# State update of a gated recurrence on Trainium2: 48 columns in place of 64 in the stationary operand and the output

## The chip, the cores and the metric

The kernel runs on one core of one Trainium2 chip. The metric is the time of one execution on the device in microseconds (us), the median over several executions. The core has five engines that work side by side, each on an instruction stream of its own: TensorE (PE in the profile; its weight loads, LDWEIGHTS, are listed apart as PEld), VectorE (DVE), ScalarE (ACT), GpSimd (POOL) and SyncE (SP), which here issues the DMA transfers. TensorE multiplies a stationary operand, which a load puts into its array, by a moving operand that streams through it, and writes to PSUM, a small memory that the other engines read from.

## The reference

Two layers follow each other: a gated linear recurrence over 4 batches, 8 heads, 768 tokens and head size 48, and a feed-forward block with a hard-swish gate.

```python
def _attn_ref(q, k, v, alpha):          # each (4, 8, 768, 48)
    for t in range(S):
        state = alpha[:, :, t, :, None] * state + np.einsum('bhd,bhe->bhde', k[:, :, t], v[:, :, t])
        y[:, :, t] = np.einsum('bhd,bhde->bhe', q[:, :, t], state)
    return y

def _moe_ref(x, w_in, w_out):           # x (3072, 384), w_in (384, 2048), w_out (2048, 384)
    h = x @ w_in
    g = h * np.clip(h + 3.0, 0.0, 6.0) / 6.0
    return g @ w_out
```

The state of each head is a 48 x 48 matrix. Everything is float32.

## The kernel before, in words

**Chunks.** The recurrence is worked in 24 chunks of 128 tokens (6 per batch, numbered j). Within a chunk the running products of alpha are folded into q and k, so that a chunk needs only matrix products: scores of q against k within each half of 64 tokens (`scores`, line 346), their product with v and the contribution of the state carried in (`attend`, line 455), and the update of the state by the chunk's k and v (`update`, line 429).

**Two heads to a tile.** The 128 partitions of the k and q tiles hold two heads: head a of a pair occupies rows 64a to 64a+47, and the 16 rows behind it are padding, with k zero there. There are NP = 4 pairs p. `kb_t[j]` is k turned round: 128 tokens on the partitions, and for each pair 128 columns, which are again 48 columns of head 0, 16 of padding, 48 of head 1 and 16 of padding. For the first chunks the turning is done by TensorE (`k_by_token`, line 374, copied by ScalarE in line 378), later by a DVE block transpose and a trip through DRAM (`turn_k`, `write_k`, `read_k`, lines 388 to 405; buffer `far`).

**The update.** `update(j, *at)` computes u = k^T v for each half b of the chunk's tokens, each pair p and each head a. The stationary operand is 64 tokens x 64 columns of `kb_t[j]`, the moving operand is 64 tokens x 48 columns of v, and the output goes to 64 partitions of a PSUM bank, one bank per half. A call issues 16 such products (8 in the last chunk of each batch, where only one half is needed). They use a quarter of the array each: rows 64b to 64b+63 and columns 64a to 64a+63, written 64*64 in the profile. Since the operands are float32, each product becomes two weight loads and two matmuls: 32 of each per call, 704 of each in all.

**What reads u.** `next_state(j, b)` (line 439, line 437 for the first half of a batch) adds u, read over all 128 partitions, to the state on VectorE: first to `half_st` (named s in the profile), then to `sm`. Only rows 64a to 64a+47 of the states are read after that: `place_state` (line 419) copies them beside v, where `attend` uses them. `decayed_state` (line 409, GpSimd) makes `st` out of `sm`.

**The feed-forward block.** It works on groups of two chunks, 256 tokens. The first groups use plain products (`ff1`, line 478; `ff1_half`, line 489; `ff2`, line 516). Later ones use schemes with fewer products and more additions: `product1` (line 600) and `product` (line 703) on TensorE, with the sums before and after on VectorE (lines 537 to 541, 647, 664, 723), copies on ScalarE (lines 606, 682, 709) and the gate on both (lines 494 and 498).

**Order.** The whole order is written out by hand in one string of steps (from line 755), such as `u.16.0.3` for the update of chunk 16 into banks 0 and 3; nothing is reordered by a scheduler. Each engine takes its instructions in that order and waits on semaphores where a buffer or an operand isn't ready.

Of the kernel before, what the change touches and what calls it, by code (L numbers as in the profile page):

```python
# [17 lines left out]
def kernel(  # L18
# [32 lines left out]
    nc = tc.nc  # L51
    B, H, S, D = q.shape
# [26 lines left out]
    half = consts.tile([C, 1], FP, tag="half")  # L79
# [141 lines left out]
    R_t, P_t, Q_t, K_t, kb_t, A_t, xT_t, ps_t = ({} for _ in range(8))  # L221
# [200 lines left out]
    def update(j, *at):  # L422
        for b, i in enumerate(at):
            ps_t["u", j, b] = banks[i][:, 0 : NP * D].rearrange("r (p n) -> r p n", p=NP)
        for p in range(NP):
            for a in range(2):
                for b in range(len(at)):
                    half = slice(HB * b, HB * b + HB)
                    nc.tensor.matmul(ps_t["u", j, b][64 * a : 64 * a + 64, p],  # L429
                                     kb_t[j][half, p, 64 * a : 64 * a + 64],  # L430
                                     v_t[j][half, b, 2 * p + a, 0:D],
                                     start=True, stop=True)

# [189 lines left out]
    def hidden1(g, o):  # L623
# [16 lines left out]
    b = {(i, k): w2[:, i * HF : (i + 1) * HF, k * HD : (k + 1) * HD]  # L640
         for i in range(2) for k in range(2)}
# [83 lines left out]
    def store2(g, i):  # L725
# [13 lines left out]
        "sc": scores, "m": masked, "qa": place_q, "kb": k_by_token, "ck": keep_k,  # L739
        "st": decayed_state, "sv": place_state, "kt": turn_k, "kw": write_k, "kr": read_k,  # L740
        "u": update, "sm": next_state, "ya": lambda j, i: attend(j, 0, i),
        "yb": lambda j: attend(j, 1), "cy": keep_x,
        "f": ff1, "fa": lambda i, m: ff1_half(0, i, m), "fb": lambda i: ff1_half(1, i, None), "fr": gate, "fg": hidden, "b": ff2, "bo": keep_out, "so": store, "x": combine_w2,
# [195 lines left out]
```

## Time and profile before

| | us |
|---|---|
| median of 3 executions | 539.71 (539.61 to 539.85) |
| profiled execution, first to last instruction (the span) | 538.1 |
| median less this span | 1.6 |
| line 429, matmuls, busy (704) | 16.7 |
| line 429, weight loads, busy (704) | 14.2 |
| line 346, matmuls, busy (768) | 16.7 |
| line 455, matmuls, busy (1536) | 25.5 |
| line 600, matmuls, busy (1600) | 209.1 |
| line 703, matmuls, busy (1232) | 213.7 |

The profile shows one execution; of the time outside its span nothing is recorded. Busy time is the union of the records of a group, so records that overlap are counted once: a matmul of line 429 lasts some 220 ns from the start of its record to the end, but 704 of them take up only 16.7 us, since many are in flight at the same time. The spacing of starts, not the length of one, tells how fast they follow each other. The granted TensorE clock is 1.0 throughout.

### The profile page before, as it was taken

What the parts mean: (1) busy time and instruction counts of PE and PEld (TensorE: products, weight loads), DVE (VectorE), ACT (ScalarE), POOL (GpSimd) and SP (SyncE); (2) the same over time, 40 slices, a digit from 0 to 9 for tenths busy, and PEclk for the clock granted to TensorE, in tenths of its full rate; (3) what the DMA queues carried; (4) which work ended last, traced back from release to release, by engine and by line L of the source; (5) the groups of instructions that cost most, each with busy time, mean ns of one, the idle gap of its engine ahead of it and who ended that gap; (6) DMA issues with size and microseconds to landing.
All of it is one profiled execution on the core that took longest, in us unless ns stands there. A gap on an engine that the chain in (4) does not pass through costs nothing.

```text
span 538.1 us, 15166 instructions
## 1 busy us (share of the span) xinstructions
PE 526.3 (98%) x6306; PEld 499.7 (93%) x6306; DVE 475.3 (88%) x839; ACT 259.6 (48%) x513; POOL 50.4 (9%) x71
## 2 busy tenths in 40 slices
PE   8799999999999999999999999999999999999997
PEld 7688886789999999999999999999999999999996
DVE  6999989999999899989999898999999898495481
ACT  3889865212653553543544444642644544553230
POOL 5333425100000000000010000000000000000000
PEclk9999999999999999999999999999999999999999
DMA  9998876006625156263444355155354042100001
GB/s 172 211 251 250 218 217 154 17 2 154 149 35 117 30 117 141 46 140 86 94 109 112 89 121 137 21 127 120 88 136 103 15 103 42 44 3 1 15 16 37
DMA packets 124101, 54.40 MB, mean 101 GB/s; under 512 B 83329, under 2 KB 116865, under 8 KB 124033
## 3 DMA queue, kind: packets, MB, share of 16 engines
q1 hardware_dynamic: 124032, 53.44, 43.7%
q8 instruction: 49, 0.80, 0.7%
q14 instruction: 20, 0.16, 0.1%
HBM read 44.50 MB, written 8.91 MB: 99 GB/s over the span
## 4 chain that ended last, share of the span: by engine, by line
PE 83%; DVE 10%; DMA 3%; ACT 1%; issue 1%; SPq 0%; POOL 0%; DVEq 0%; ACTq 0%; POOLq 0%
PE m_ps L703 32%; PE m_ps L600 32%; PE m_ps L478 6%; PE t_ps L455 4%; PE t_ps L346 2%; PE t_ps L429 2%; DMA v<-in_v_dram 2%; PE m_ps L532 1%; PE m_ps L489 1%; PE m_ps L516 1%; DVE rings L647 1%; DVE R L309 1%; DVE raw L537 1%; DVE g_sb L647 1%; DVE w L537 1%
## 5 line engine op out<-in xcount | busy, mean ns | idle before, releaser
L703 PE MATMUL m_ps<-w,g_sb 128*128 128x192 f32 x704 | 122.1, 327 | 0.6 <-ACT m_ps L709 0.5
L606 ACT COPY g_sb<-m_ps 128x512 f32<-128x512 f32 x110 | 63.5, 584 | 114.7 <-PE m_ps L600 98.2
L703 PEld LDWEIGHTS m_ps<-w,g_sb 128*128 128x128 f32 x704 | 113.7, 190 | 1.7 <-ACT m_ps L709 0.8
L703 PE MATMUL m_ps<-rings,g_sb 128*128 128x192 f32 x528 | 91.6, 327 | 0.6 <-ACT u L682 0.6
L703 PEld LDWEIGHTS m_ps<-rings,g_sb 128*128 128x128 f32 x528 | 85.3, 190 | 1.0 <-ACT u L682 0.9
L600 PE MATMUL m_ps<-xc,w 128*128 128x128 f32 x640 | 82.7, 277 | 0.2 <-DVE w L541 0.2
L600 PEld LDWEIGHTS m_ps<-xc,w 128*128 128x128 f32 x640 | 77.5, 192 | 1.4 <-issue 0.4
L494 ACT ACTIVATE r<-g_sb,half 128x512 f32<-128x512 f32 x80 | 56.7, 722 | 29.4 <-DVE g_sb L541 11.7
L498 DVE SCALAR_TENSOR_TENSOR g_sb<-r,g_sb 128x512 f32<-128x512 f32 x80 | 53.6, 682 | 7.5 <-ACT r L494 7.0
L600 PE MATMUL m_ps<-xT,raw 128*128 128x128 f32 x400 | 52.6, 278 | 0.9 <-ACT g_sb L606 0.9
L600 PEld LDWEIGHTS m_ps<-xT,raw 128*128 128x128 f32 x400 | 48.6, 192 | 1.9 <-ACT g_sb L606 1.2
L409 POOL TENSOR_TENSOR st<-sm,R 128x192 f32<-128x192 f32 x20 | 12.9, 643 | 355.8 <-DVE sm L439 306.7
L647 DVE TENSOR_TENSOR g_sb<-g_sb 128x512 f32<-128x512 f32 (+1 forms) x55 | 42.0, 792 | 1.4 <-PE m_ps L703 1.1
L600 PE MATMUL m_ps<-xT,w 128*128 128x128 f32 x320 | 42.0, 276 | 0.0
L600 PEld LDWEIGHTS m_ps<-xT,w 128*128 128x128 f32 x320 | 39.3, 192 | 0.1
L366 ACT COPY A<-q 48x256 f32<-48x256 f32 x88 | 35.6, 404 | 4.9 <-DVE q L332 3.7
L356 DVE TENSOR_TENSOR A<-t_ps,mask 64x256 f32<-64x256 f32 x96 | 36.1, 414 | 0.4
L478 PE MATMUL m_ps<-xT,w 128*128 128x256 f32 x144 | 32.8, 382 | 0.0
L600 PE MATMUL m_ps<-xc,raw 128*128 128x128 f32 x240 | 31.8, 276 | 0.0
L309 DVE TENSOR_TENSOR_SCAN R<-t,ones 128x516 f32<-128x516 f32 x24 | 29.5, 1231 | 1.3 <-ACT t L300 1.2
L478 PEld LDWEIGHTS m_ps<-xT,w 128*128 128x128 f32 x144 | 26.7, 190 | 3.6
L600 PEld LDWEIGHTS m_ps<-xc,raw 128*128 128x128 f32 x240 | 29.6, 192 | 0.1
(105 smaller groups left out, 730.0 us busy)
## 6 DMA issues: line engine op xcount, KB each, us to landing
raw<-in_moe_w_out_dram SPq DMA_DIRECT2D x8, 768.0 KB, 4.8
raw<-in_moe_w_in_dram SPq DMA_DIRECT2D x6, 768.0 KB, 7.0
v<-in_v_dram SPq DMA_DIRECT2D x48, 96.0 KB, 3.2
out_dram<-oh SPq DMA_DIRECT2D x44, 96.0 KB, 1.8
far<-kq SPq DMA_DIRECT2D x64, 64.0 KB, 2.2
kb<-far SPq DMA_DIRECT2D x64, 64.0 KB, 2.0
aq<-in_alpha_dram SPq DMA_DIRECT2D x36, 96.0 KB, 2.6
qq<-in_q_dram SPq DMA_DIRECT2D x36, 96.0 KB, 2.5
```

The costliest lines, as they stand in the source:

```text
L309: nc.vector.tensor_tensor_scan(out=reverse(R, n - 1, n), data0=reverse(ax, n, n), data1=reverse(ones, n, n), initial=0.0, op0=ALU.mult, op ...
L356: nc.vector.tensor_tensor(out=to[:, a], in0=sc[a][half], in1=mask[half, half].unsqueeze(1).to_broadcast([HB, NP, HB]), op=ALU.mult)
L366: nc.scalar.copy(out=to[:, a], in_=Q_t[j][64 * a : 64 * a + D, :, half])
L409: nc.gpsimd.tensor_tensor(out=st, in0=sm, in1=R_t[j][:, :, 0:1].to_broadcast([C, NP, D]), op=ALU.mult)
L455: nc.tensor.matmul(y_of(j, (i + 1) // 2, p)[:, HB * b : HB * b + HB], vb[:, p, e : e + 32], A_t[j][:, b, 2 * p + a], start=(b == 0 and i = ...
L478: nc.tensor.matmul(h[:, f], w1[:, kk, o : o + C], xT_t[g][:, kk], start=(kk == 0), stop=(kk == KT - 1))
L494: nc.scalar.activation(out=to, in_=h, func=AF.Relu, bias=half, scale=1.0 / 6.0)
L498: nc.vector.scalar_tensor_tensor(out=to, in0=r, scalar=1.0, in1=h, op0=ALU.min, op1=ALU.mult)
L600: nc.tensor.matmul(acc[g][i][:, f * C : (f + 1) * C], spots[w][:, f * C : (f + 1) * C], x_of(g, x), start=(first and f == 0), stop=last, s ...
L606: nc.scalar.copy(out=slots[z], in_=acc[g][i])
L647: nc.vector.tensor_tensor(out=out, in0=in0, in1=in1, op=ALU.subtract)
L703: nc.tensor.matmul(to[g], a, rhs[:, f], start=(first and f == 0), stop=(last and f == HF - 1), skip_group_check=True)
```

## The change

In `update`, the stationary operand becomes 48 of the 64 columns, and the output 48 of the 64 partitions. The moving operand, the number of products, their order, the array quarter that each uses and every other line are as before.

```diff
@@ -426,8 +426,8 @@
             for a in range(2):
                 for b in range(len(at)):
                     half = slice(HB * b, HB * b + HB)
-                    nc.tensor.matmul(ps_t["u", j, b][64 * a : 64 * a + 64, p],
-                                     kb_t[j][half, p, 64 * a : 64 * a + 64],
+                    nc.tensor.matmul(ps_t["u", j, b][64 * a : 64 * a + D, p],
+                                     kb_t[j][half, p, 64 * a : 64 * a + D],
                                      v_t[j][half, b, 2 * p + a, 0:D],
                                      start=True, stop=True)
```

D is 48. The 16 partitions behind each head keep in PSUM what an earlier product left there; `next_state` still reads and adds them, and nothing reads those rows of the state.

## The prediction, made before the changed kernel ran

> **What bounds the kernel now.** I read the page first: engine shares, then the chain of work that ended last.
>
> ```profile
> PE 526.3 (98%) x6306; PEld 499.7 (93%) x6306; DVE 475.3 (88%) x839; ACT 259.6 (48%) x513; POOL 50.4 (9%) x71
> ...
> PE 83%; DVE 10%; DMA 3%; ACT 1%; issue 1%; SPq 0%; POOL 0%; DVEq 0%; ACTq 0%; POOLq 0%
> ```
>
> TensorE is busy nearly always, and 83% of the chain is its work. A shorter TensorE instruction is therefore worth something, provided that it lies on the chain and that its spacing, not only its length, gets shorter. The busy time by stretch says where VectorE could take over (columns: stretch, its length, then busy us and count of each engine, clock, DMA share, GB/s):
>
> ```profile
> 90.00:130.00 40.00, 39.77 (x332) 32.54 (x331) 39.72 (x63) 9.47 (x23) 2.50 (x4) 1.00 0.22 50
> 130.00:190.00 60.00, 59.84 (x855) 58.16 (x854) 57.40 (x107) 31.79 (x66) 2.92 (x4) 1.00 0.41 92
> ...
> 200.00:282.00 82.00, 82.00 (x1042) 80.42 (x1041) 77.97 (x141) 37.89 (x80) 2.68 (x4) 1.00 0.46 103
> 282.00:440.00 158.00, 157.10 (x2049) 154.29 (x2049) 148.48 (x271) 73.71 (x158) 5.04 (x9) 1.00 0.43 97
> ```
>
> From 90 to 130 us VectorE is full (39.72 of 40.00 us), and there the chain runs on it. From 130 to 440 us TensorE is full and VectorE has 4 to 6% left (77.97 of 82.00, 148.48 of 158.00).
>
> Then the changed line, by groups (operands as array rows*columns and out partitions x moving columns; busy us, mean ns of one), with the two lines nearest to it in shape:
>
> ```profile
> L346 PE MATMUL t_ps<-q,k 48*64 48x64 f32 x768 | 16.7, 223 | 0.1
> L429 PE MATMUL t_ps<-v,kb 64*64 64x48 f32 x704 | 16.7, 220 | 1.8 <-ACT kb L378 1.0 <-DMA v<-in_v_dram 0.5 <-issue 0.3
> ...
> L455 PEld LDWEIGHTS t_ps<-A,v 128*32 128x32 f32 x1536 | 22.4, 110 | 3.8 <-DVE s L439 1.0 <-issue 0.7 <-ACT A L366 0.6
> L429 PEld LDWEIGHTS t_ps<-v,kb 64*64 64x64 f32 x704 | 14.2, 134 | 4.3 <-issue 2.9 <-DMA v<-in_v_dram 0.7
> ```
>
> A load of 32 columns lasts 110 ns, one of 64 lasts 134, and one of 128 (line 703) lasts 190: 0.8 ns a column, so the load's length goes by columns.
>
> Last, two calls in the chain in order of time (start, us, what):
>
> ```profile
> 201.21 0.62 PE t_ps L346 x32
> 201.83 0.45 PE t_ps L429 x32
> 202.29 1.76 PE m_ps L600 x14
> ...
> 324.95 0.61 PE t_ps L429 x32
> 325.56 0.48 PE t_ps L346 x32
> ```
>
> The update sits in the chain between other TensorE work, with no wait on either side: what it loses in length, the next line starts earlier.
>
> **The change, part by part.** It adds and removes no instruction and no wait and moves none; on DVE, ACT, POOL and SP nothing differs. The 704 loads of line 429 bring 48 columns instead of 64, and the 704 matmuls have 48 output columns of the array active. `next_state` reads the same 128 partitions, so its 0.35 us stays.
>
> *What one round costs now.* I looked at the single records of the call at 324.88 us. Matmuls start in bursts of four, 6.6 ns apart (one for each quarter of the array), and a burst follows the one before after 58.4 ns: the first of each start at 324.975, 325.033, 325.092, 325.150, ... 325.325, six rounds in 350 ns. With 32 matmuls a call has 8 rounds. The one-half calls (16 matmuls, two quarters) have 8 rounds of 58.4 ns too, so the round belongs to a quarter's own load and matmul, not to the number in flight.
>
> *What sets the 58.4 ns.* Rows with one array quarter, column strip or whole array give spacings by the single records: moving 192 columns 162.7 ns (line 703), 256 columns 216 (line 478), 384 columns 323 (line 516). That is 0.835 ns a column plus 2.5, and gives 56 for 64 columns: line 455, with moving 64 and loads of 32, shows 55.9. Line 346 has the same 64 moving columns but loads of 64, and its round is 58.4. Line 429 moves only 48 columns, for which the matmul line gives 42.5, and its round is 58.4 as well. Line 600 moves 128 (109.5 by the matmul line) and loads 128: 111.7. So two rows that share loads of 64 share 58.4, and loads of 128 give 111.7: (111.7 - 58.4) / 64 = 0.833 ns a column plus 5. I take the load as what sets line 429's round. A load of 48 then gives 40 + 5 = 45.0 ns, just above the matmul's 42.5. Each round saves 13.3 ns, each call 8 x 13.3 = 107 ns.
>
> *Bounds of that saving, since no row has a load of 48.* Best: the round falls to the matmul's 42.5, 15.9 ns x 8 = 127 ns a call; for that the load's 5 ns would have to vanish, which lines 346 and 600 both show. Worst among the harmless ends: a load of 48 costs as one of 64, 0 ns. I take 107, on the line through 64 and 128, from which 48 is 16 columns away.
>
> *How many calls count.* Of the 24 calls, the chain holds 19: those near 34, 45 and 73 us, and 16 from 142 to 468 us. Not in it are 13, 20, 95, 110 and 446 us, where the chain runs on DVE, DMA or ACT. Where it leaves TensorE after 130 us (190 us, over a v load issue and a k transfer through DRAM; 438 us, over ScalarE's copy, a store and the read of k), it does so from a TensorE instruction, so what was saved up to there is carried across, if the transfers start earlier with their issue. The three early calls feed the stretch from 93 to 128 us that VectorE fills; I count them half. Sum: 16 x 107 + 3 x 53 = 1.71 + 0.16 = 1.87 us. The profiled span of 538.1 becomes 536.2; the median shown, 1.6 us above that span, becomes 537.8.
>
> *What hides the rest.* The five calls off the chain are costed at nothing, covered by VectorE's sums (95, 110), by waits for transfers and small DVE work (13, 20) and by ScalarE (446). Were that cover absent, they would add 5 x 107 = 0.53 us. VectorE is next in line: from 130 to 440 us it has 4 to 6% free and the edit takes 15 x 0.107 = 1.6 us, 0.5%, from TensorE's time there, so it doesn't become the bound on average.
>
> **The rivals.**
>
> *Issue sets the round, no gain or almost none.* Line 455 sustains 256 records (loads and matmuls) at 55.9 ns for eight, 7.0 ns a record, and no row keeps a faster pace for long; a round of 45.0 would need 5.6. If 55.9 is a floor, a call saves 2.5 x 8 = 20 ns, 19 calls 0.38 us: 539.3. If the load is rounded to its 64-column quarter: 539.7. For it: no row of this kernel goes below 55.9. Against it: 55.9 is just what 64 moving columns explain, and within a burst eight records start in some 27 ns, 3.4 ns each. The Trainium skill ("TensorE: Matmul & The Clock Gate", sections "Wait — 56ns, not 53.3ns?" and "Back-to-back issue gap") has a rule of this kind: matmul starts never come closer than about 25 ns, however few columns. By that rule over the whole engine 32 matmuls would take an estimated 800 ns a call and narrower loads would bring nothing, 539.7; this trace has 32 starts in 0.46 us and 6.6 ns within a burst, so the rule can only hold for one quarter of the array, where 45 ns is above it.
>
> *The stops outside TensorE take it back.* If the transfer at 190 us (3.16 us in the chain) and the one at 440 us (1.75 us) landed at times of their own, only the call at 468 us would stay: 539.6. Their issue stands behind instructions that wait for TensorE, and DMA shares are 0.51 and 0.23 there, which speaks against it.
>
> *Slower: a partly filled strip breaks the overlap of the quarters.* 48 columns fill one 32-column strip and half of another. If two quarters that share rows could then no longer load side by side, a round would hold two loads, 2 x 45 = 90 ns, 32 more than now: 8 x 32 x 19 calls = 4.8 us, 544.5. It decides as soon as a round is above 58.4 ns. Nothing in the trace has a partial column count; line 346 has partial rows (48 of 64) and keeps its overlap, which speaks weakly against.
>
> **How the numbers follow.** Forecast, the load by columns: 0.76, 537.8, with its own range from 537.0 (all 24 calls at 107 ns and the early ones whole is 2.56; somewhat more with the bound of 127) to 538.6 (six tenths of the 1.87 carried). Issue or rounding: 0.11, 539.3 to 539.7. Stops: 0.05, 539.6. Slower: 0.08, 544.5. 0.2% is 1.1 us, about what a measurement of this kernel can tell from no change: faster by more is the first case, 0.76; within is the second and third, 0.16; slower is 0.08. The range 537.0 to 539.7 reaches over the first three cases.
>
> **What would show it.** Right: bursts of line 429 some 45 ns apart, its loads near 121 ns (134 less 13), its matmuls' busy time down by some 24 x 0.107 = 2.5 us to about 14, line 346 after it starting 0.1 us sooner, the groups of all other lines unchanged. Rounds at 55.9 or 58.4 would show the issue or rounding rival; rounds of 45 with a span unchanged and new TensorE idle time near 190 or 440 us, the stops; bursts of two instead of four, the slower one. The forecast is wrong if the round isn't load-bound, or if VectorE fills the time in the stretches after 130 us.

## The result, and the profile after

| | before, us | changed, us |
|---|---|---|
| median, 5 executions each, side by side | 539.71 (539.52 to 540.30) | 537.66 (537.36 to 537.83) |
| profiled execution, span | 538.1 | 535.6 |

The ratio is 0.9969, with a 95% interval of 0.9959 to 0.9980: faster by 1.1 to 2.2 us. (The ratio is an estimate of its own and not the quotient of the two medians, which differ by 2.05 us.) The forecast was 537.8. Two more measurements of the changed kernel, each beside new executions of the kernel before, gave ratios of 0.9967 (0.9955 to 0.9980) and 0.9968 (0.9956 to 0.9980).

The page's engine shares of the changed kernel:

```profile
PE 523.6 (98%) x6306; PEld 497.0 (93%) x6306; DVE 475.1 (89%) x839; ACT 259.7 (48%) x513; POOL 50.4 (9%) x71
```

TensorE's busy time fell by 2.7 us; the other engines kept theirs. The groups by line, matmuls and weight loads:

```profile
L346 PE MATMUL t_ps<-q,k 48*64 48x64 f32 x768 | 16.6, 223 | 0.0
L429 PE MATMUL t_ps<-v,kb 64*48 64x48 f32 x704 | 14.2, 208 | 1.4 <-issue 1.0 <-ACT kb L378 0.3 <-DMA v<-in_v_dram 0.2
...
L429 PEld LDWEIGHTS t_ps<-v,kb 64*48 64x48 f32 x704 | 11.7, 121 | 4.1 <-issue 2.9 <-DMA v<-in_v_dram 0.3
```

Line 429 takes 14.2 us where it took 16.7, its loads last 121 ns where they lasted 134, and line 346 is as it was. So 2.5 of the 2.7 us are line 429's own. In the single records of its full calls after 100 us, bursts of four matmuls follow each other at 45.0 ns (median of 15 calls), 58.3 before.

The call that stood at 324.88 us, in the order of time (start, us, engine, line), first the kernel before, then the changed one, weight loads only:

```profile
324.88 0.56 PEld L429 LDWEIGHTS t_ps<-v,kb 64*64 64x64 f32 x32
325.34 0.56 PEld L346 LDWEIGHTS t_ps<-q,k 48*64 48x64 f32 x32
325.97 0.97 PEld L600 LDWEIGHTS m_ps<-xT,raw 128*128 128x128 f32 x8
```

```profile
323.06 0.45 PEld L429 LDWEIGHTS t_ps<-v,kb 64*48 64x48 f32 x32
323.41 0.56 PEld L346 LDWEIGHTS t_ps<-q,k 48*64 48x64 f32 x32
324.05 0.97 PEld L600 LDWEIGHTS m_ps<-xT,raw 128*128 128x128 f32 x8
```

From the update's first load to the first load of line 600, 1.09 us became 0.99: 0.10 us a call, and the next line takes it up at once.

Not all of it reaches the end. TensorE's waits that grew, in order of time, first the kernel before, then the changed one (in brackets: idle time before the work, and what ended it):

```profile
128.94 0.46 PE L600 MATMUL m_ps<-xc,w 128*128 128x128 f32 x2 [0.23 <-DVE w L541]
...
446.51 0.76 PE L703 MATMUL m_ps<-w,g_sb 128*128 128x192 f32 x3 [0.35 <-ACT m_ps L709]
```

```profile
127.84 1.13 PE L600 MATMUL m_ps<-xc,w 128*128 128x128 f32 x8 [0.47 <-DVE w L541]
...
444.07 2.87 PE L703 MATMUL m_ps<-w,g_sb 128*128 128x192 f32 x16 [0.45 <-ACT m_ps L709]
```

At the end of the stretch that VectorE fills, TensorE waits 0.24 us longer, and at 444 us 0.10 us longer for a copy by ScalarE. A third wait, 0.12 us between the records of line 429 and line 600 at 239.8 us, is new; the chain of the changed kernel there runs over a copy by ScalarE (line 606). Two later profiles of the changed kernel have the same three waits (0.45 to 0.46, 0.10 and 0.43 to 0.44 us). Comparing the starts of the calls in the two profiles, the lead of the changed kernel grows from 1.25 us at the call near 110 us to 2.44 us at the one near 445: 1.19 us over 16 calls, where 16 x 0.107 would be 1.71. Between most neighbouring calls it grows by 0.08 to 0.11 us; what is missing was lost between 110 and 142 us (0.26), around the wait for VectorE, and around 240 us (0.14), with small change between.

Most of the lead of 1.25 us at 110 us need not be the change's: of it, 0.9 us comes at once at the call near 34 us. There the first profile of the kernel before has its wait for v, and the changed kernel has none. The experiments below had to say whether the narrower calls cause that.

### The profile page after: what moved, and what is told of

Same layout as the page of the kernel before. It is cut to its first block, busy times and chain, and to the rows that moved or that the text cites. A ratio compares the mean times of both kernels' runs of the same rounds, so it can differ in the third digit from the quotient of the medians.

```text
span 535.6 us, 15166 instructions
## 1 busy us (share of the span) xinstructions
PE 523.6 (98%) x6306; PEld 497.0 (93%) x6306; DVE 475.1 (89%) x839; ACT 259.7 (48%) x513; POOL 50.4 (9%) x71
## 4 chain that ended last, share of the span: by engine, by line
PE 64%; DVE 20%; SPq 5%; DMA 3%; issue 3%; ACT 2%; POOL 2%; DVEq 0%; ACTq 0%; POOLq 0%
PE m_ps L703 28%; PE m_ps L600 24%; PE m_ps L478 4%; SPq L262 3%; PE t_ps L455 3%; DVE R L309 2%; DVE g_sb L498 2%; DVE A L356 2%; DMA v<-in_v_dram 1%; PE t_ps L346 1%; PE m_ps L516 1%; PE t_ps L429 1%; DVE g_sb L537 1%; DVE q L332 1%; DVE t L286 1%
```

## The experiments

**Late and early calls apart.** The calls from chunk 7 on (142 us and later) in the first, those up to chunk 6 in the second, beside a second profile of the kernel before.

```diff
-  ... [64 * a : 64 * a + 64, p] ...                        # output, and the same in kb_t[j]
+  ... [64 * a : 64 * a + (D if j > 6 else 64), p] ...      # late only
+  ... [64 * a : 64 * a + (64 if j > 6 else D), p] ...      # early only
```

> The 48 columns only in the 17 update calls from chunk 7 on (142 us and later); the 7 early calls keep 64. Theory (every call on the chain gives its 8 rounds of 13.3 ns, 107 ns): the 16 late calls of the chain give up to 1.71 us, and as the changed kernel's trace shows between the calls at 110 and 468 us, where its lead grows by 1.2 us, more likely 1.2 to 1.5: a ratio near 0.9975. Rival (most of the gain comes from the early part, where the changed kernel's lead jumps by 0.9 us at the call near 34 us): 0.5 us or less, a ratio above 0.999.

> The 48 columns only in the 7 update calls up to chunk 6 (before 130 us); the others keep 64. Theory: half of the three early calls of the chain, 0.16 us, and up to 0.6 us if all seven count: a ratio of 0.999 to 1. Rival: the jump of 0.9 us at the call near 34 us is caused by the narrower calls, and the ratio is near 0.998.

> The kernel before, unchanged, profiled once more. Theory: the wait of 0.5 us inside the call near 34 us, and the transfer of 7.0 us ahead of it in the chain, vary from one execution to the next, so that the lead of 0.9 us there is partly chance: this profile's span lies between 537.2 and 538.1 us, and the starts of its early calls differ from the first profile's by up to a microsecond. Rival: they agree within 0.2 us.

Measured: late only 537.67 us, ratio 0.9963 (0.9949 to 0.9976); early only 538.84, ratio 0.9990 (0.9982 to 0.9999); the kernel before 539.27 in the median of 21 executions. The late calls alone reach the changed kernel's time within the measurement, and the early ones bring some 0.4 us (0.1 to 1.0). The rivals forecast a ratio above 0.999 for the late calls and near 0.998 for the early ones; both lie outside the intervals, the second only just. The theory's 1.2 to 1.5 us for the late calls lies inside the interval (1.3 to 2.7 us) only at its upper end; the medians differ by 1.6. In the profile of late only, the lead over the first profile of the kernel before grows by 1.5 us from the call near 142 us to the end.

The second profile of the kernel before has a span of 537.7 us, inside what was expected, and its early calls start up to 0.7 us sooner than the first one's. It has no wait at 34 us, but it loses time ahead of it. By stretch (columns as in the table above; the clock is the third last), first this second profile, then the first:

```profile
22.00:24.00 2.00, 1.99 (x65) 1.82 (x66) 2.00 (x4) 1.31 (x3) 1.31 (x1) 0.50 0.97 142
24.00:26.00 2.00, 2.00 (x13) 2.00 (x14) 1.66 (x4) 1.95 (x3) 2.00 (x2) 0.65 0.88 147
```

```profile
22.00:24.00 2.00, 1.64 (x68) 1.36 (x68) 2.00 (x5) 1.91 (x5) 1.25 (x1) 1.00 1.48 202
24.00:26.00 2.00, 1.89 (x16) 1.56 (x15) 1.96 (x5) 2.00 (x3) 2.00 (x2) 1.00 1.38 156
```

In one execution of the same program the granted clock is 0.50 for 3.4 us (all of the first stretch and, at a mean of 0.65, 1.4 us of the second); in the other a v transfer comes late. At the call near 45 us the two profiles stand 0.64 and 1.08 us behind the changed kernel's, of which the three calls before it can explain 0.3 at most. Neither delay is confined to one number of columns. Such a stretch at 0.50 leaves a mean clock of 0.997, and 5 of 16 executions of the changed kernel show that value. The profile of the kernel with 40 columns in every call (the last experiment below) has the same late transfer, and no lead at 45 us. First the kernel before, then the one with 40 columns:

```profile
34.35 0.67 PE L429 MATMUL t_ps<-v,kb 64*64 64x48 f32 x30 [0.53 <-DMA v<-in_v_dram]
```

```profile
34.80 0.54 PE L429 MATMUL t_ps<-v,kb 64*40 64x48 f32 x30 [1.11 <-DMA v<-in_v_dram]
```

Over 42 further executions the span of the kernel before runs from 536.8 to 538.7 us, in 25 of them from 537.0 to 537.5. The first profile, 538.1, was a long one; so an estimated 0.6 to 0.9 of the 2.5 us between the two profiled spans was chance.

**One head of two.** Only head 1 of each pair narrow.

```diff
-  ... [64 * a : 64 * a + 64, p] ...
+  ... [64 * a : 64 * a + (D if a else 64), p] ...
```

> Head 1 of each pair with 48 columns, head 0 with 64. Theory (each array quarter keeps a round of its own, and a call ends with its slowest quarter): rounds of the two quarters of head 0 stay at 58.4 ns, the call keeps its length, and the gain is 0 to 0.3 us, a ratio of 0.9995 to 1. Rival (the four loads share one path, and the round is the sum of what they bring): the round falls by half as much, to 51.7 ns, and the gain is about 1 us, a ratio near 0.998.

Measured: 538.85 us beside 539.27, ratio 0.9991 (0.9982 to 0.9999), by the medians 0.4 us, less than half of the whole change's gain. The single records settle it: in the call near 362 us, the matmuls of 48 columns follow each other in pairs at 45 ns and are done after 0.36 us, those of 64 at 58.4 ns over 0.45 us, in the same call. Each quarter of the array keeps its own pace, and the call ends with the slower ones. The loads do not share one path.

**56 and 32 columns.** With 32, the other 16 rows of each head's state are left out.

```diff
-  ... [64 * a : 64 * a + 64, p] ...
+  ... [64 * a : 64 * a + 56, p] ...      # 56 columns
+  ... [64 * a : 64 * a + 32, p] ...      # 32 columns
```

> Stationary operand and output of 56 columns in every call. Theory (the load by columns, linear): a round of 46.7 + 5 = 51.7 ns, half of the changed kernel's saving, about 1 us, a ratio near 0.998. Rival (the load goes by steps of 16 or 32 columns): a round of 58.4 ns and no gain.

> Stationary operand and output of 32 columns in every call; the other 16 rows of each head's state are left out. Theory: at 48 columns the load (45.0 ns) stands just above the matmul of 48 moving columns (42.5 ns), so with a load of 31.7 ns the matmul sets the round: 42.5 ns, 20 ns a call less than the changed kernel, in all 0.3 to 0.5 us less. Rival (the load alone sets the round): 31.7 ns, 107 ns a call less than the changed kernel, in all about 2 us less. Rival (a floor of the issue near 45 ns): no change from the changed kernel.

> The changed kernel once more, on the same chip as the two others of this call. Theory: a gain of 1.6 to 2.1 us, a ratio of 0.996 to 0.997; the starts of its early calls vary from the first profile's as those of the kernel before do.

Measured beside 539.04 us of the kernel before: 56 columns 538.58, ratio 0.9989 (0.9981 to 0.9998), bursts 51.7 ns apart; the changed kernel 537.43, ratio 0.9967 (0.9955 to 0.9980); 32 columns 538.49, ratio 0.9986 (0.9977 to 0.9995), bursts 42.5 ns apart. The round with 56 columns falls on the line for loads (46.7 + 5), so a load that goes by steps of 16 or 32 columns is ruled out. The time with 56 columns fell short, though: the medians differ by 0.46 us (0.1 to 1.0 by the interval) where about 1 was expected. In its trace the lead grows by 0.60 us between the calls near 110 and 445 us, half of the changed kernel's 1.19, so the late calls do as expected. Part of the rest is the clock: six of its eleven executions have the mean of 0.997. The spans of the other five have a median of 536.5 us, 0.7 below the kernel before at a clock of 1.00 (537.2), where the changed kernel, beside it, is 1.5 below. The round with 32 columns falls on the matmul's 42.5, as the theory said. But the time went the wrong way: 1.1 us above the changed kernel, where 0.3 to 0.5 less was expected. The order of time shows where, TensorE matmuls of the 32-column kernel first, then of the changed one:

```profile
199.66 0.69 PE L346 MATMUL t_ps<-q,k 48*64 48x64 f32 x32
200.29 0.55 PE L429 MATMUL t_ps<-v,kb 64*32 64x48 f32 x32
200.76 1.16 PE L600 MATMUL m_ps<-xT,raw 128*128 128x128 f32 x8
```

```profile
199.78 0.69 PE L346 MATMUL t_ps<-q,k 48*64 48x64 f32 x32
200.29 0.54 PE L429 MATMUL t_ps<-v,kb 64*48 64x48 f32 x32
200.76 1.16 PE L600 MATMUL m_ps<-xT,raw 128*128 128x128 f32 x8
```

The update starts 0.63 us after line 346 instead of 0.51. By the single records, from the last matmul of line 346 to the second burst of line 429 it is 216 ns with 32 columns and in most calls 85 with 48; where line 346 follows line 429, 240 against 97. The explanation proposed is that a stationary operand of 32 columns is placed in a strip of 64 x 32 of the array, while line 346 uses quarters of 64 x 64, so that the array has to be divided anew between the two. The profile names the columns (64*32) but not the placing. The Trainium skill ("TensorEngine Tiling (Array Packing)", section Key Properties) says that a change of the tiling mode, not of the tile alone, drains TensorE. The 130 to 143 ns more at each change fit that; the trace shows the pause, not a drain. With 48 or 56 columns line 429 follows line 346 as in the kernel before (85 ns). There are 17 such neighbours after 35 us, and 17 x 0.135 = 2.3 us is an estimate from above, since in some calls the changed kernel pauses there too (171 ns near 180 and 379 us). Against it stand 24 x 0.02 = 0.5 us saved by the rounds: up to 1.8 us more if all lay on the path, 1.1 measured.

**40 columns**, to tell the division of the array from the number of columns; 8 rows of each head's state are left out.

```diff
-  ... [64 * a : 64 * a + 64, p] ...
+  ... [64 * a : 64 * a + 40, p] ...
```

> Stationary operand and output of 40 columns in every call; the other 8 rows of each head's state are left out. 40 columns still lie in an array quarter of 64 x 64, where 32 columns had taken a strip of 64 x 32. Theory (the larger of load and matmul sets the round; 32 columns lost by the change of the array's division between line 346 and line 429): the load is 33.3 + 5 = 38.3 ns, the matmul of 48 moving columns 42.5, so a round of 42.5 ns, line 429 following line 346 without a stop, and a time 0.3 to 0.5 us under the changed kernel. Rival (with fewer than 48 columns something else in the array slows the calls down, and the division isn't the cause): a time above the changed kernel's, as with 32 columns.

> The changed kernel a third time, beside the one with 40 columns on the same chip. Theory: a ratio of 0.996 to 0.997, and 0.3 to 0.5 us above the one with 40 columns.

Measured beside 539.03 us: 40 columns 537.18, ratio 0.9970 (0.9959 to 0.9982); the changed kernel 537.35, ratio 0.9968 (0.9956 to 0.9980). The bursts are 42.5 ns apart, and from line 346 to the second burst of line 429 it is 85 ns: the pause is gone, although fewer columns are used than in the changed kernel, and the rival falls. So the pause comes with 32 columns and not with 40, as the explanation by the array's division says; a second cause that sets in between 40 and 32 columns isn't excluded. The medians differ by 0.17 us, under the expected 0.3 to 0.5 and inside the intervals, and by the ratios the changed kernel is ahead; that the matmul's 2.5 ns a round are worth something at the end is not shown.

No run beat the changed kernel while computing all of it. The load's round, at 45.0 ns, is now 2.5 ns above the 42.5 at which the round stops falling.

## Why the prediction was right

**The round.** 45.0 ns was worked out from loads of 64 and 128 columns and a constant of 5 ns; 45.0 was measured, and 51.7 at 56 columns. The loads' length (121 ns), line 429's busy time (14.2 us for "about 14") and the unchanged line 346 came as stated.

**The bound.** That the load and not the matmul set the round of 58.4 rested on two rows. The runs with 40 and 32 columns show both limbs of it: below 48 columns the round stays at 42.5, the value of the matmul's line for 48 moving columns. No run moves fewer columns, so a floor of one quarter's pace at just this value would look the same.

**How many calls count.** The sum gave 1.71 us to the 16 late calls and 0.16 to the early ones. Measured apart they brought 1.6 us (1.3 to 2.7) and 0.4 us (0.1 to 1.0) by the medians, and both intervals hold the forecast. The traces are finer: from the call near 142 us, the first late one, to the end of the span, the changed kernel gains 1.4 us on the first profile of the kernel before, and the one with late calls alone 1.5. So by the traces "carried across" was too generous by 0.2 to 0.3 us; of these, 0.12 and 0.10 went into the waits near 240 and 444 us, where a copy by ScalarE ends last. The 0.24 us longer wait for VectorE at 128 us comes before the first late call and takes back lead from the early ones, as the prediction's half for those calls supposed. The early term may have been too small by about as much as the late one was too large. That the two come out near the measured whole is in part luck, and the medians can't tell them apart.

**What was not seen.** The statement that VectorE does not become the bound holds in busy time, but the chain has changed more than was foreseen. The chain of the changed kernel by engine:

```profile
PE 64%; DVE 20%; SPq 5%; DMA 3%; issue 3%; ACT 2%; POOL 2%; DVEq 0%; ACTq 0%; POOLq 0%
```

TensorE's share of the chain fell from 83% to 64%, with VectorE at 20% and SyncE's issuing at 5%, though TensorE is busy for 98% of the span as before. Several paths of almost equal length lie side by side; which of them the chain follows says little about what a further cut is worth. The new chain around 130 us (start, us, what):

```profile
132.57 0.43 SPq L262
133.05 0.43 SPq L262
133.52 0.43 SPq L262
133.99 1.98 DMA aq<-in_alpha_dram
135.98 0.65 DVE g_sb L537
136.62 1.03 DVE k L286
```

SyncE issues one transfer after another at 0.43 us each, and the chain passes from the last of them to VectorE. But VectorE's own records show no idle time above 0.04 us from 126 to 142 us in either profile, so the transfer held nothing up there. Whether a further cut on TensorE would meet this path, no run shows.

**The rivals.** Issue as the bound falls: 64 records in eight rounds of 45.0 ns are 5.6 ns a record, sustained, and 42.5 ns makes 5.3. The one-half calls, with half as many records to a round, keep the same rounds (45.0 with 48 columns, 42.5 with 40 and 32), so the round doesn't go by the number of records. The Trainium skill's floor of about 25 ns between matmul starts ("TensorE: Matmul & The Clock Gate", section "Wait — 56ns, not 53.3ns?") can't hold over the whole array here, where a start comes every 11 ns on average within a call; for one quarter no run went below 42.5, so it was not tested there. The stops outside TensorE took back 0.1 us at 444 us, not the whole. The slower rival falls: with 56, 48 and 40 columns, which don't fill whole strips of 32, the bursts stay bursts of four and the rounds are shorter. The cost that did turn up, with 32 columns, is a pause between two lines and no loss of overlap within a call.

**The baseline.** The sum was made against a profile whose span lay near the top of what this kernel shows. It did no harm, since the saving was worked out by calls and the sum taken off the median. That median, 539.71, was itself a high one: beside the experiments the kernel before had 539.27, 539.04 and 539.03.

## What to carry to other kernels

Where small float32 products run side by side in parts of the array, look at the spacing of the starts within one part and set it beside the line for loads and the line for moving columns: the larger one is what a narrower operand can lower, and the smaller one is where it stops. Cut padding columns, and look at the pause between neighbouring lines too: here 32 columns, half of the width that the neighbouring products use, cost 130 to 143 ns at each change of line, where the shorter rounds saved 20 ns a call. When a gain of a few tenths of a per cent is read from two profiles, split it by position first: here about a third of the difference between the spans was chance, with one late transfer in it.

## What the runs showed of the hardware

Where the load sets the round, it goes by the load's columns: 58.4, 51.7 and 45.0 ns at 64, 56 and 48 columns, on one line, with no step at 16 or 32. Two quarters of the array with different loads keep different paces, 45 and 58.4 ns, in the same stream of instructions. Between neighbouring lines of 64 x 64 quarters, products with 32 columns brought a pause of 130 to 143 ns that products with 40 to 64 columns did not. The granted clock fell to 0.50 for 3.4 us from 22 us on in one execution and stayed at 1.00 there in another of the same program; what makes it fall, no run shows.
